# A decode step on one core: projections and output rows summed by weighted adds on ScalarE and DVE, the first K in halves

## The chip, the core and the metric

The kernel runs on one core of one Trainium2 chip. It computes one decoding step: a layer norm, attention with 32 heads over a cache of 16384 keys, and a gated GELU block beside it, for a batch of one. The metric is the device time of one execution in microseconds (us), the median over runs. All data is fp32.

## The reference

```python
xn = layernorm(x)                                   # x: 1 x 576
q = (xn @ wq).reshape(32, 128)                      # wq: 576 x 4096
scores = q_h . k_cache[h] * 128 ** -0.5             # k_cache: 32 x 16384 x 128
o_h = softmax(scores_h) @ v_cache[h]                # v_cache: 32 x 16384 x 128
attn = concat(o_h) @ wo                             # wo: 4096 x 576
h = gelu_tanh(xn @ w_gate) * (xn @ w_up)            # both 576 x 4608
out = x + attn + h @ w_down                         # w_down: 4608 x 576
```

The caches are 268 MB each, the five weight matrices together some 51 MB.

## The kernel before

There are three large SBUF slots of 64 KB in each partition: `sa`, `sb` and `sv` (slot_a, slot_b and slot_v in the profile). One head's K or V fills a slot: partition p holds 128 keys of 128 numbers each. All large transfers are issued on SP's queue, in program order; a transfer into a slot waits there until the slot's readers are done, and so does everything behind it on SP. The class `Order` works out the semaphore waits of the parts that are not in loops from the byte ranges that instructions read and write; an instruction of DVE waits for an earlier one of DVE too where the two share bytes that one of them writes. The helpers `pe_op` (L207), `dve` (L210), `act` (L215) and `load` (through L107) record those instructions, so all of them carry these lines in the profile.

**Start.** The 576 rows of a projection lie as four rows of 128 partitions (row j of partition p is weight row 4p+j) and a tail of 64 weight rows, each split in two over 128 partitions. SP loads wq (into `sa`), its tail (`sb`), then row 3 and the tail of w_gate and of w_up (`sv`), then the other three rows of w_gate (`sb`), of w_up (`sa`, after the q projection), K of head 0 (`sb`), K of head 1 (`sa`) and V of head 0 (`sv`). `project` multiplies on PE: the normalised x, copied to 32 columns, is the stationary operand, one step for each of the four rows and the tail, accumulated in PSUM. q takes 40 matmuls, w_gate and w_up 60 each. `ffn` then takes the diagonal parts out of PSUM with DVE (`tensor_mul` with `same`, `tensor_reduce`) and `ffn_act` makes `hT`, the 4608 hidden numbers as 128 x 36.

**Heads.** For each head DVE multiplies K by q in place (L382), reduces over the 128 numbers of a key (L384), and finds the maximum with PE's help (L387, L389); ScalarE takes the exponent; PE multiplies by V (L329, 32 matmuls). DVE's mul and reduce free K's slot for K two heads later, PE's end frees V's slot for the next V.

**Tail.** w_down lies as 36 rows of 576 numbers in each partition, wo as 32. `WD_A` = 28 rows of w_down go to `sb` once head 30's K has been used; V of head 31 is issued behind them; once head 31's K has been used, 8 more rows of w_down and the first 20 rows of wo go to `sa`, and 12 rows of wo to `sb`, in the pieces of `WO_PIECES`. DVE adds the 28 rows, each times a column of `hT`, into one row `total`: one `tensor_scalar` and 27 `scalar_tensor_tensor`, each on the result of the one before. PE multiplies `total` by ones, the other 8 rows by columns of `hT`, and the 32 rows of wo by columns of `oT`, the normalised attention output; the first 24 rows of wo go in two halves of 288 columns, the last 8 in four quarters of 144. x comes in through `x2`. A copy by DVE (`o4`) and four small stores end the kernel.

Of the kernel before, what the change touches and what calls it, by code (L numbers as in the profile page):

```python
# [9 lines left out]
AF = mybir.ActivationFunctionType  # L10
ALU = mybir.AluOpType
# [19 lines left out]
WD_A = 28  # L31
WO_PIECES = (8, 12, 4, 4, 2, 1, 1)
WO_A = 20
WO_Q = 8
QUART = D // 4
SLOT_AT = 27904
# [117 lines left out]
def decode(tc, x, k_cache, v_cache, wq, wo, wg, wu, wd, out, slots, s_ends):  # L154
    nc = tc.nc
    o = Order(tc)
    places = [e.mark_branch_hint_location() for e in (nc.vector, nc.scalar)]
# [29 lines left out]
    x2 = sbuf("x2", P, HALF)  # L187
# [4 lines left out]
    lsum, oall = sbuf("lsum", P, H), sbuf("oall", P, H + 1)  # L192
# [4 lines left out]
    oT = sbuf("oT", P, WO_T)  # L197
    assert nc.sbuf_base <= SLOT_AT, nc.sbuf_base

# [13 lines left out]
    def act(out, src, func=AF.Copy, signal=None, **kw):  # L213
        also = [kw["accum_out"]] if "accum_out" in kw else []
        o.op("scalar", lambda e: e.activation(out, src, func, **kw), out, src, kw.get("bias") if isinstance(kw.get("bias"), bass.AP) else None, also=also, signal=signal)  # L215
# [5 lines left out]
    ROW3 = 3 * DF  # L221
    nc.tensor.wait_ge(s_ends, 64).then_inc(s_ends, -64)
    qt = load(sb[:, ROW3 : ROW3 + QS], wtail["q"])
    row3, tails, at = {}, {}, 0
    for n in "gu":
        row3[n] = load(sv[:, at : at + DF], wmain[n][:, ROW3:])
        tails[n] = load(sv[:, at + DF : at + DF + DF // 2], wtail[n])
        at += DF + DF // 2

    xrow = sv[:1, ROW3 + FG : ROW3 + FG + D]  # L230
    load(xrow, xf, eng="scalar")
    o.op("gpsimd", lambda e: e.memset(x2, 0.0), x2)
    for i in range(2):
        load(x2[32 * i : 32 * i + 1, :], xf[:, i * HALF : (i + 1) * HALF], eng="scalar")
# [5 lines left out]
    s_q, s_m, s_n, s_o, s_e, s_v, s_po, s_pq, s_pt, s_pb, s_pc, s_vf, s_kf, s_qf, s_qd, s_d, s_a = (  # L240
        tc.alloc_semaphore(f"h{n}") for n in range(17))
    s_k = [tc.alloc_semaphore(f"k{n}") for n in range(2)]
    for bank, s in ((PO, s_po), (pc, None), (pq, None)):
        o.op("vector", lambda e, bank=bank: e.memset(bank, 0.0), bank, signal=s)
# [15 lines left out]
    for j in range(DJ):  # L260
        pe_op(pc[:, j : j + 1], xm[:, j, :], ones[:1, :1], True, True)
    xd = sv[:1, ROW3 + 2 * FG : ROW3 + 2 * FG + 2 * (D - DM)]
    dve("tensor_copy", xd.rearrange("o (d s) -> o d s", s=2), xrow[:, DM:].unsqueeze(2).to_broadcast([1, D - DM, 2]))
    pe_op(pc[:, DJ : DJ + 1], xd, ones[:1, :1], True, True)
    xp = small[:, 26 : 26 + DJ + 1]
    dve("tensor_copy", xp, pc[:, : DJ + 1])
    xnb, xtb = z[:, : DJ * 32], z[:, DJ * 32 : DJ * 32 + 64]
    dve("tensor_copy", xnb.rearrange("p (j r) -> p j r", j=DJ), xp[:, :DJ].unsqueeze(2).to_broadcast([P, DJ, 32]))
    xt = tt[:, :2]
    dve("tensor_scalar", xt, par, xp[:, DJ:], None, op0=ALU.mult)  # L270
    dve("tensor_copy", xtb.rearrange("p (s r) -> p s r", s=2), xt.unsqueeze(2).to_broadcast([P, 2, 32]))

    def project(dst, steps, group, sizes):
        for k, (j, rhs) in enumerate(steps):
            for b, size in enumerate(sizes):
                for q in range(4):
                    lo = q * group + sum(sizes[:b])
                    if j < DJ:
                        lhs = xnb[:, 32 * j : 32 * j + 32]
                    else:  # L280
                        lhs = xtb[:, 32 * (q // 2) : 32 * (q // 2) + 32]
                        lo -= q // 2 * 2 * group
                    pe_op(dst[32 * q : 32 * q + 32, 512 * b : 512 * b + size], lhs, rhs[:, lo : lo + size],
                          k == 0, k == len(steps) - 1)

    project(qb, [(DJ, qt)] + [(j, sa[:, j * HD : (j + 1) * HD]) for j in range(DJ)], QG, (QB, QB))
# [10 lines left out]
    def ffn(which):  # L297
        n, t = "gu"[which], (sb, sa)[which]
        steps = [(3, row3[n]), (DJ, tails[n])]
        load(t[:, :ROW3], wmain[n][:, :ROW3])  # L300
        project(pg, steps + [(j, t[:, j * DF : (j + 1) * DF]) for j in range(DJ - 1)], FG, FB)
        gm = sv[:, ROW3 : ROW3 + FG].rearrange("p (m t) -> p m t", t=WD_T)
        at = 0
        for b, size in enumerate(FB):
            m = size // WD_T
            dve("tensor_mul", gm[:, at : at + m, :], pg[:, 512 * b : 512 * b + size].rearrange("p (m t) -> p m t", t=WD_T),
                same[:, at : at + m].unsqueeze(2).to_broadcast([P, m, WD_T]))
            at += m
        dve("tensor_reduce", gu[:, which * WD_T : (which + 1) * WD_T], gm.rearrange("p m t -> p t m"), axis=AX.X, op=ALU.add)

    ffn(0)
    ffn(1)

# [10 lines left out]
    def out_steps(h):  # L324
        return [(pc[:, :1], z[:, j * DH : (j + 1) * DH], same[:, j : j + 1], j == 0, j == 3) for j in range(4)]
# [12 lines left out]
    ffn_act()  # L338
    o.wait("tensor", [ident, ones, same], [pg, pc, PO, pq])
    o.wait("vector", [qs], [S, pm, nm])  # L340
    o.wait("scalar", [qb], [z, qs, nb, pe, lsum, oall, qcur])

# [6 lines left out]
    for h, dst in ((0, sb), (1, sa)):  # L349
        o.wait("sync", [], [dst])  # L350
        load_k(h, dst, h)
# [9 lines left out]
    with nc.Fori(0, H, engines=OrderedEngineSet([KIND["tensor"]]), head_slot={KIND["tensor"]: 0}):  # L361
# [6 lines left out]
        take(nc.tensor, s_o)  # L368
        chain(out_steps(0), s_pc)
# [4 lines left out]
        nc.tensor.drain().then_inc(s_vf, 1)  # L374

    with nc.vector.Fori(0, H // 2):
        for s, kt in ((0, sb), (1, sa)):
            blk = kt.rearrange("p (n d) -> p n d", d=DH)
            sc = S[:, s * R : s * R + R]
            take(nc.vector, s_k[s], 16)  # L380
            take(nc.vector, s_qd)
            nc.vector.tensor_mul(blk, blk, qs.unsqueeze(1).to_broadcast([P, R, DH])).then_inc(s_d, 1)  # L382
            nc.vector.wait_ge(s_d, 1).then_inc(s_qf, 1)
            nc.vector.tensor_reduce(sc, blk, axis=AX.X, op=ALU.add).then_inc(s_d, 1)  # L384
            nc.vector.wait_ge(s_d, 2).then_inc(s_kf, 1)
            take(nc.vector, s_d, 2)
            nc.vector.reduce_max(pm, sc, axis=AX.X).then_inc(s_m, 1)  # L387
            take(nc.vector, s_pt)
            nc.vector.tensor_reduce(nm[:1], pt[:1, :P], axis=AX.X, op=ALU.max, negate=True).then_inc(s_n, 1)  # L389

    for h0, n in ((0, 6), (6, 8), (14, 8), (22, 8), (30, 2)):
        row, lo = divmod(min(h0 + 2, H - 1), H // 4)
        with nc.scalar.Fori(0, n) as i:
            take(nc.scalar, s_po)
            nc.scalar.activation(z, PO, AF.Copy).then_inc(s_o, 1)  # L395
# [7 lines left out]
            take(nc.scalar, s_pc)  # L403
            nc.scalar.activation(oall[:, bass.ds(i + h0, 1)], pc[:, :1], AF.Copy)
            src = q_part(min(h0 + 2, H - 1)) if n == 2 else qb[32 * row : 32 * row + 1, bass.ds(i * DH + lo * DH, DH)]
            nc.scalar.activation(qcur, src, AF.Copy).then_inc(s_q, 1)

# [5 lines left out]
    first = load_rows(sb, 0, wdv, 0, WD_A)  # L413
    total = first[0]
    dve("tensor_scalar", total, total, hT[:, 0:1], None, op0=ALU.mult)
    for j in range(1, WD_A):
        dve("scalar_tensor_tensor", total, first[j], hT[:, j : j + 1], total, op0=ALU.mult, op1=ALU.add)
# [3 lines left out]
    wd_rows = load_rows(sa, 0, wdv, WD_A, WD_T - WD_A)  # L421
    wo_rows, lo = [], 0
    for n in WO_PIECES:
        wo_rows += load_rows(sa, WD_T - WD_A + lo, wov, lo, n) if lo < WO_A else load_rows(sb, 1 + lo - WO_A, wov, lo, n)
        lo += n

    take(nc.scalar, s_po)
    act(z, PO)
    o.note("scalar", o.sem["scalar"], o.count["scalar"], [pc, pq, pb, PO, qb], [oall, lsum])
    for s in out_steps(H - 1):  # L430
        pe_op(*s)
    act(oall[:, H:], pc[:, :1])

# [4 lines left out]
    dve("tensor_mul", on, oall[:, 1:], rl)  # L438
# [6 lines left out]
    seen = set()  # L445
    pairs = (qb[:, :512], qb[:, 512:])
    acc4 = pg[:, :QUART]
    half = [[pairs[i][32 * (2 * i + j) : 32 * (2 * i + j) + 1, :HALF] for j in range(2)] for i in range(2)]
    quart = [acc4[32 * g : 32 * g + 1, :] for g in range(4)]

    def add_out(groups, lhs, w, last=False):
        n = D // len(groups)
        for i, g in enumerate(groups):
            pe_op(g, lhs, w[:, i * n : (i + 1) * n], id(g) not in seen, last)
            seen.add(id(g))

    turn = 0
    for w, lhs in [(w, hT[:, WD_A + j : WD_A + j + 1]) for j, w in enumerate(wd_rows)] + [(total, ones[:, :1])]:
        add_out(half[turn % 2], lhs, w)
        turn += 1  # L460
    for j, w in enumerate(wo_rows):
        if j < WO_T - WO_Q:
            add_out(half[turn % 2], oT[:, j : j + 1], w, last=j >= WO_T - WO_Q - 2)
            turn += 1
            continue
# [42 lines left out]
```

## Time and profile before

| | |
|---|---|
| median of 3 runs | 1365.26 us (1364.94 to 1365.76) |
| the profiled execution's own time | 1364.84 us |
| its span, first to last instruction | 1363.0 us |
| DVE busy | 1158.4 us, 85% |
| PE busy | 446.3 us, 33% |
| ScalarE busy | 67.8 us, 5% |
| mean granted TensorE clock | 0.629 of full speed |
| HBM read | 587.60 MB |

The span leaves out 1.84 us of the profiled execution's time, so a span is compared with a span, and 1.84 us and the distance to the median are added at the end. Times of day in the text are us from the start of the span. In a timeline row the first number is the start, the second the length; the brackets at its end hold the idle time of the engine before it and what ended that. Rows with xN stand for N instructions. PE records two matmuls for one fp32 matmul. SPq rows are the issues of transfers, not the transfers.

### The profile page before, as it was taken

The page shows a single profiled execution, that of the slowest core. Times are in us where ns is not written, and L with a number is a line of the kernel's source. Part 1 is how long each engine was busy: PE and PEld are TensorE (multiplying, and loading weights), DVE is VectorE, ACT ScalarE, POOL GpSimd, SP SyncE. Part 2 cuts the span into 40 slices and gives each one's busy share as a digit, 9 for nine tenths or more (in the row PEclk, how much of TensorE's full clock was granted, in tenths as well). Part 3 has the DMA queues.
Part 4 walks back from the last instruction along what each step waited for, and adds up shares of the span by engine and source line. Part 5 has one row for each costly group of instructions (what it writes and reads, how often), then busy time and mean ns, then how long its engine had stood idle before and what let it go on. Part 6 is the DMA issues. An engine that isn't in the chain of part 4 may idle for free. (4 is left out here: it accounts for less than half of the span.)

```text
span 1363.0 us, 7778 instructions
## 1 busy us (share of the span) xinstructions
PE 446.3 (33%) x3012; PEld 161.7 (12%) x3012; DVE 1158.4 (85%) x193; ACT 67.8 (5%) x234; POOL 1.0 (0%) x7
## 2 busy tenths in 40 slices
PE   2431233333322333323222333333223333232236
PEld 1110101111111111101111111011011111011112
DVE  1049999999998888898888888998888888988882
ACT  0000000000000000000000000000000000000000
POOL 0000000000000000000000000000000000000000
PEclk9675666666556666665566666665566666655568
DMA  9999999999999999999999999999999999999998
GB/s 401 446 424 431 431 440 437 431 435 431 435 437 431 433 431 431 446 435 431 431 439 433 433 431 431 446 435 431 431 435 437 433 431 431 444 437 431 430 437 349
DMA packets 11683, 587.69 MB, mean 431 GB/s; under 512 B 1303, under 2 KB 1309, under 8 KB 1694
## 3 DMA queue, kind: packets, MB, share of 16 engines
q1 hardware_dynamic: 11668, 587.60, 99.7%
q8 instruction: 5, 0.08, 0.0%
q10 hardware_dynamic: 10, 0.01, 0.0%
HBM read 587.60 MB, written 0.00 MB: 431 GB/s over the span
## 5 line engine op out<-in xcount | busy, mean ns | idle before, releaser
L329 PE MATMUL po<-slot_v,pe 128*4 128x512 f32 x2048 | 291.7, 733 | 532.6 <-PEq L333 532.6
L382 DVE TENSOR_TENSOR slot_b<-slot_b,qs 128x16384 f32<-128x16384 f32 x16 | 275.6, 17226 | 38.0 <-DVEq L333 38.0
L382 DVE TENSOR_TENSOR slot_a<-slot_a,qs 128x16384 f32<-128x16384 f32 x16 | 275.6, 17226 | 30.6 <-DVEq L333 30.6
L384 DVE TENSOR_REDUCE scores<-slot_a 128x128 f32<-128x16384 f32 x16 | 275.5, 17220 | 2.3
L384 DVE TENSOR_REDUCE scores<-slot_b 128x128 f32<-128x16384 f32 x16 | 275.5, 17220 | 2.3
L329 PEld LDWEIGHTS po<-slot_v,pe 128*4 128x4 f32 x2048 | 56.2, 98 | 740.9 <-issue 740.9
L365 PE MATMUL pg<-ident,pm 128*1 128x128 f32 x32 | 11.9, 371 | 287.3 <-PEq L333 287.3
L329 PE MATMUL pc<-same,z 128*128 128x1 f32 x256 | 59.8, 355 | 0.0
L395 ACT ACTIVATE z<-po 128x512 f32<-128x512 f32 x32 | 19.1, 597 | 783.1 <-ACTq L333 783.1
L329 PEld LDWEIGHTS pc<-same,z 128*128 128x128 f32 x256 | 57.1, 328 | 0.5
L210 DVE TENSOR_TENSOR slot_v<-pg,same 128x396 f32<-128x396 f32 (+1 forms) x6 | 3.3, 558 | 51.9 <-PE pg L207 51.7
L365 PEld LDWEIGHTS pg<-ident,pm 128*1 128x1 f32 x32 | 2.5, 79 | 292.6 <-issue 292.6
L389 DVE TENSOR_REDUCE nm<-pg 1x1 f32<-1x128 f32 x32 | 8.9, 279 | 21.5 <-DVEq L333 21.5
L329 PE MATMUL pg<-nm,ones 1*128 1x1 f32 x64 | 17.7, 343 | 18.5 <-PEq L333 18.5
L329 PE MATMUL pqs<-qcur,ones 1*128 1x128 f32 x64 | 14.8, 312 | 25.3 <-PEq L333 25.3
L210 DVE SCALAR_TENSOR_TENSOR slot_b<-slot_b,hT 128x576 f32<-128x576 f32 x27 | 22.1, 819 | 0.9
L400 ACT ACTIVATE nb<-pg 128x1 f32<-128x1 f32 x32 | 5.5, 171 | 292.3 <-ACTq L333 292.3
L329 PEld LDWEIGHTS pg<-nm,ones 1*128 1x128 f32 x64 | 15.9, 306 | 27.9 <-issue 27.9
L387 DVE TENSOR_REDUCE pm<-scores 128x1 f32<-128x128 f32 x32 | 9.1, 286 | 8.2 <-DVEq L333 8.2
L329 PEld LDWEIGHTS pqs<-qcur,ones 1*128 1x128 f32 x64 | 9.6, 186 | 53.9 <-issue 53.9
L207 PE MATMUL pg<-slot_b,z 128*32 128x396 f32 (+1 forms) x72 | 8.8, 661 | 17.5 <-DMA slot_b<-in_B_w_gate_dram 17.5
L402 ACT ACTIVATE pe<-scores,nb 128x128 f32 x32 | 12.8, 401 | 9.6 <-ACTq L333 9.6
(79 smaller groups left out, 115.3 us busy)
## 6 DMA issues: line engine op xcount, KB each, us to landing
slot_b<-in_B_w_down_dram SPq DMA_DIRECT2D x1, 8064.0 KB, 42.0
slot_b<-in_B_w_gate_dram SPq DMA_DIRECT2D x1, 6912.0 KB, 54.9
slot_a<-in_B_w_up_dram SPq DMA_DIRECT2D x1, 6912.0 KB, 38.2
slot_a<-in_A_wo_dram SPq DMA_DIRECT2D x1, 3456.0 KB, 41.0
slot_v<-in_B_w_gate_dram SPq DMA_DIRECT2D x1, 2304.0 KB, 28.8
slot_v<-in_B_w_up_dram SPq DMA_DIRECT2D x1, 2304.0 KB, 36.8
slot_a<-in_B_w_down_dram SPq DMA_DIRECT2D x1, 2304.0 KB, 28.1
slot_a<-in_A_wo_dram SPq DMA_DIRECT2D x1, 2304.0 KB, 33.2
```

Source lines behind the costliest of these rows:

```text
L207: o.op("tensor", lambda e: e.matmul(outp, lhsT, rhs, start=start, stop=stop), outp, lhsT, rhs, signal=signal)
L210: o.op("vector", lambda e: getattr(e, name)(out, *ins, **kw), out, *[a for a in ins if isinstance(a, bass.AP)], *[a for a in kw.values() i ...
L329: i = nc.tensor.matmul(dst, lhs, rhs, start=start, stop=stop)
L365: nc.tensor.transpose(pt[:1, :P], pm, ident).then_inc(s_pt, 1)
L382: nc.vector.tensor_mul(blk, blk, qs.unsqueeze(1).to_broadcast([P, R, DH])).then_inc(s_d, 1)
L384: nc.vector.tensor_reduce(sc, blk, axis=AX.X, op=ALU.add).then_inc(s_d, 1)
L387: nc.vector.reduce_max(pm, sc, axis=AX.X).then_inc(s_m, 1)
L389: nc.vector.tensor_reduce(nm[:1], pt[:1, :P], axis=AX.X, op=ALU.max, negate=True).then_inc(s_n, 1)
L395: nc.scalar.activation(z, PO, AF.Copy).then_inc(s_o, 1)
L400: nc.scalar.activation(nb, pb[:, :1], AF.Copy, scale=SCALE).then_inc(s_a, 1)
L402: nc.scalar.activation(pe, S[:, bass.ds(i % 2 * R, R)], AF.Exp, bias=nb, scale=SCALE, accum_out=lsum[:, bass.ds(i + h0, 1)]).then_inc(s_e, 1)
```

## The change

The projections are summed by weighted adds: ScalarE (`weigh`) scales one of the four rows in place by its column of x, DVE (`gather`) adds the other rows and the two halves of the tail onto it, and PE only sums over partitions, with `ones` as the stationary operand (8 matmuls for q, 12 each for w_gate and w_up). ScalarE copies the result out of PSUM into `gm` (`unfold`), DVE takes the diagonal there (`fold`). w_gate's three rows are issued ahead of w_up's row 3 and tail; w_up's three rows come in two transfers. K of head 0 comes in two halves, and DVE works on each; `fold(1)` and `ffn_act` come behind head 0's reduces. DVE's loop covers heads 1 to 30, and head 31 stands behind it.

In the tail `WD_A` is 20, and 16 further rows of w_down come in two pieces of 8 behind V of head 31. DVE adds all 36 rows of w_down and 22 of the 32 rows of wo, in turn into two accumulators `totals`; PE takes eight rows of wo in halves (`WO_HALF`), which DVE adds to `totals[1]`, and the last two rows, with the sum of the totals, in quarters. x comes in through `xres`.

In PE's loop `out_steps` moves behind the 32 matmuls with V, and ScalarE's copies `z` and `oall` move to the end of its loop. PE gets a branch hint and a `release` as DVE and ScalarE had.

```diff
-WD_A = 28
-WO_PIECES = (8, 12, 4, 4, 2, 1, 1)
-WO_A = 20
-WO_Q = 8
+WD_A = 20
+WD_B = (8, 8)
+WO_PIECES = (4, 8, 8, 4, 4, 2, 1, 1)
+WO_A = 12
+WO_HALF = (5, 7, 9, 11, 13, 15, 17, 19)
+WO_QUART = 2
...
-    nc.tensor.wait_ge(s_ends, 64).then_inc(s_ends, -64)
...
+        if n == "g":
+            load(sb[:, : 3 * DF], wmain[n][:, : 3 * DF])
...
+    def weigh(total, j):
+        act(total, total, scale=xp[:, j : j + 1])
+
+    def gather(total, steps):
+        for j, row in steps:
+            n = row.shape[1]
+            for s in range(2) if j == DJ else (0,):
+                part = total[:, s * n : (s + 1) * n]
+                col = xt[:, s : s + 1] if j == DJ else xp[:, j : j + 1]
+                dve("scalar_tensor_tensor", part, row, col, part, op0=ALU.mult, op1=ALU.add)
+
+    def project(dst, total, group, sizes):
+        for b, size in enumerate(sizes):
+            for q in range(4):
+                lo = q * group + sum(sizes[:b])
+                pe_op(dst[32 * q : 32 * q + 32, 512 * b : 512 * b + size], ones[:, :32], total[:, lo : lo + size], True, True)
...
+    nc.scalar.wait_ge(s_ends, 64).then_inc(s_ends, -64)
+    weigh(qrows[0], 0)
+    gather(qrows[0], [(j, qrows[j]) for j in range(1, DJ)] + [(DJ, qt)])
+    project(qb, qrows[0], QG, (QB, QB))
+    weigh(rows["g"][0], 3)
...
+    gather(rows["g"][0], [(DJ, tails["g"])] + [(j, rows["g"][1 + j]) for j in range(3)])
+    project(pg, rows["g"][0], FG, FB)
+    weigh(rows["u"][0], 3)
+    unfold(0)
+    gather(rows["u"][0], [(DJ, tails["u"])])
+    fold(0)
+    gather(rows["u"][0], [(j, rows["u"][1 + j]) for j in range(3)])
+    project(pg, rows["u"][0], FG, FB)
+    unfold(1)
...
+    for src, sc in parts:
+        blk = src.rearrange("p (n d) -> p n d", d=DH)
+        dve("tensor_mul", blk, blk, qs.unsqueeze(1).to_broadcast([P, SUB, DH]))
+        dve("tensor_reduce", sc, blk, axis=AX.X, op=ALU.add)
...
+    fold(1)
+    ffn_act()
...
-    first = load_rows(sb, 0, wdv, 0, WD_A)
+    wd_rows = load_rows(sb, 0, wdv, 0, WD_A)
     take(nc.sync, s_vf)
     load_v(H - 1)
     take(nc.sync, s_kf)
+    for n in WD_B:
+        wd_rows += load_rows(sa, len(wd_rows) - WD_A, wdv, len(wd_rows), n)
+    totals, turn = wd_rows[:2], 0
+
+    def add_row(row, col):
+        nonlocal turn
+        total, turn = totals[turn % 2], turn + 1
+        if total is row:
+            dve("tensor_scalar", total, row, col, None, op0=ALU.mult)
+        else:
+            dve("scalar_tensor_tensor", total, row, col, total, op0=ALU.mult, op1=ALU.add)
+
+    for j, row in enumerate(wd_rows):
+        add_row(row, hT[:, j : j + 1])
+        if j == 1:
+            dve("tensor_add", totals[0][:1], totals[0][:1], xres)
...
+    for j, row in enumerate(wo_rows):
+        col = oT[:, j : j + 1]
+        if j in WO_HALF:
+            add_out(half, col, row, j == WO_HALF[0], j == WO_HALF[-1])
+        elif j < WO_T - WO_QUART:
+            add_row(row, col)
+        if j == WO_PIECES[0] + WO_PIECES[1] + WO_PIECES[2] + WO_PIECES[3] - 1:
+            for i, g in enumerate(half):
+                part = totals[1][:1, i * HALF : (i + 1) * HALF]
+                dve("tensor_add", part, part, g)
+        if j == WO_T - WO_QUART - 1:
+            dve("tensor_add", totals[0], totals[0], totals[1])
+        if j == WO_T - 2:
+            add_out(quart, col, row, True, False)
+            add_out(quart, ones[:, :1], totals[0], False, False)
+        elif j == WO_T - 1:
+            add_out(quart, col, row, False, True)
```

More of the change, by code (lines that the diff above doesn't have):

```diff
@@ L197, in decode @@
     oT = sbuf("oT", P, WO_T)
+    gm = sbuf("gm", P, FG)
     assert nc.sbuf_base <= SLOT_AT, nc.sbuf_base
@@ L266, in decode @@
+    xp, xt = small[:, 26 : 26 + DJ + 1], tt[:, :2]
     dve("tensor_copy", xp, pc[:, : DJ + 1])
-    xnb, xtb = z[:, : DJ * 32], z[:, DJ * 32 : DJ * 32 + 64]
-    dve("tensor_copy", xnb.rearrange("p (j r) -> p j r", j=DJ), xp[:, :DJ].unsqueeze(2).to_broadcast([P, DJ, 32]))
-    xt = tt[:, :2]
     dve("tensor_scalar", xt, par, xp[:, DJ:], None, op0=ALU.mult)
[L271 to L284, printed above, removed]
@@ new lines, in project, with unfold, fold @@
+    def project(dst, total, group, sizes):
[3 more added lines that the diff above has]
+                pe_op(dst[32 * q : 32 * q + 32, 512 * b : 512 * b + size], ones[:, :32], total[:, lo : lo + size], True, True)
+    def unfold(which):
+        at = 0
+        for b, size in enumerate(FB):
+            act(gm[:, at : at + size], pg[:, 512 * b : 512 * b + size])
+            at += size
+    def fold(which):
+        g3 = gm.rearrange("p (m t) -> p m t", t=WD_T)
+        dve("tensor_mul", g3, g3, same.unsqueeze(2).to_broadcast([P, 32, WD_T]))
+        dve("tensor_reduce", gu[:, which * WD_T : (which + 1) * WD_T], gm.rearrange("p (m t) -> p t m", t=WD_T), axis=AX.X, op=ALU.add)
@@ L295, in decode @@
     act(qcur, q_part(1), signal=s_q)
[L297 to L312, printed above, removed]
+    for lo, hi in ((0, 2), (2, 3)):
+        load(sa[:, lo * DF : hi * DF], wmain["u"][:, lo * DF : hi * DF])
+    rows["u"] += [sa[:, j * DF : (j + 1) * DF] for j in range(3)]
+    gather(rows["g"][0], [(DJ, tails["g"])] + [(j, rows["g"][1 + j]) for j in range(3)])
[7 more added lines that the diff above has]
+    unfold(1)
     def ffn_act():
@@ L336, in head @@
         return bass.ds(h, 1)
[L338 to L341, printed above, removed]
     def load_k(h, dst, s):
@@ L359, in decode, with highest, scores_of @@
             load_v(i * 2 + (1 + s))
-    with nc.Fori(0, H, engines=OrderedEngineSet([KIND["tensor"]]), head_slot={KIND["tensor"]: 0}):
+    def highest(sc):
+        nc.vector.reduce_max(pm, sc, axis=AX.X).then_inc(s_m, 1)
+        take(nc.vector, s_pt)
+        nc.vector.tensor_reduce(nm[:1], pt[:1, :P], axis=AX.X, op=ALU.max, negate=True).then_inc(s_n, 1)
+    def scores_of(kt, s):
+        sc = S[:, s * R : s * R + R]
+        blk = kt.rearrange("p (n d) -> p n d", d=DH)
+        take(nc.vector, s_k[s], 16)
+        take(nc.vector, s_qd)
+        nc.vector.tensor_mul(blk, blk, qs.unsqueeze(1).to_broadcast([P, R, DH])).then_inc(s_d, 1)
+        nc.vector.wait_ge(s_d, 1).then_inc(s_qf, 1)
+        nc.vector.tensor_reduce(sc, blk, axis=AX.X, op=ALU.add).then_inc(s_d, 1)
+        nc.vector.wait_ge(s_d, 2).then_inc(s_kf, 1)
+        take(nc.vector, s_d, 2)
+        highest(sc)
+    take(nc.vector, s_qd)
+    for src, sc in parts:
+        blk = src.rearrange("p (n d) -> p n d", d=DH)
+        dve("tensor_mul", blk, blk, qs.unsqueeze(1).to_broadcast([P, SUB, DH]))
+        dve("tensor_reduce", sc, blk, axis=AX.X, op=ALU.add)
+    nc.vector.wait_ge(o.sem["vector"], o.count["vector"]).then_inc(s_kf, 1)
+    nc.vector.nop().then_inc(s_qf, 1)
+    o.wait("tensor", [ident, ones, same], [pg, pc, PO, pq])
+    o.wait("scalar", [qb], [z, qs, nb, pe, lsum, oall, qcur])
+    fold(1)
+    ffn_act()
+    o.wait("vector", [qs], [S, pm, nm])
+    highest(S[:, :R])
+    with nc.Fori(0, H, engines=OrderedEngineSet([KIND["tensor"]])):
         take(nc.tensor, s_q)
@@ L374, in decode @@
         nc.tensor.drain().then_inc(s_vf, 1)
[L376 to L389, printed above, removed]
+        take(nc.tensor, s_o)
+        chain(out_steps(), s_pc)
+    with nc.vector.Fori(0, (H - 2) // 2):
+        scores_of(sa, 1)
+        scores_of(sb, 0)
+    scores_of(sa, 1)
     for h0, n in ((0, 6), (6, 8), (14, 8), (22, 8), (30, 2)):
@@ L443, in decode, with add_out @@
     act(oT, po)
[L445 to L451, printed above, removed]
+    half = [qb[32 * i : 32 * i + 1, 512 * i : 512 * i + HALF] for i in range(2)]
+    quart = [pg[32 * i : 32 * i + 1, :QUART] for i in range(4)]
+    def add_out(groups, lhs, w, first, last):
@@ L452, in add_out @@
         n = D // len(groups)
         for i, g in enumerate(groups):
[L454 to L465, printed above, removed]
-        if j == WO_T - 4:
-            dve("tensor_add", x2[:64], x2[:64], pairs[1][64:, :HALF])
-            dve("tensor_add", x2[:64], x2[:64], pairs[0][:64, :HALF])
-            for i, g in enumerate(quart):
-                r, lo = 32 * (i // 2), i % 2 * QUART
-                pe_op(g, ones[r : r + 1, :1], x2[r : r + 1, lo : lo + QUART], False, False)
-        add_out(quart, oT[:, j : j + 1], w, last=j == WO_T - 1)
+            pe_op(g, lhs, w[:, i * n : (i + 1) * n], first, last)
```

85 lines of the change are left out of this document (36 added, 49 removed).

## The prediction

> **What bounds the kernel now.** The page comes first: the busy share of the DMA engines in 40 slices, and the queue that SP fills.
>
> ```profile
> DMA  9999999999999999999999999999999999999998
> q1 hardware_dynamic: 11668, 587.60, 99.7%
> ```
>
> The transfers are busy throughout. Whether they ever ran dry is read from landings: PE begins on a V that it waited for, and DVE on a K.
>
> ```profile
> 172.57 9.44 PE L329 MATMUL po<-slot_v,pe 128*4 128x512 f32 x64 [2.86 <-PEq L333]
> ...
> 1293.54 8.75 PE L329 MATMUL po<-slot_v,pe 128*4 128x512 f32 x64 [19.26 <-PEq L333]
> ...
> 1331.88 8.35 PE L329 MATMUL po<-slot_v,pe 128*4 128x512 f32 x64 [18.96 <-PEq L333]
> ```
>
> V of head 1 lands at 172.5, V of head 30 at 1293.5: 29 heads of 16.78 MB in 1121.0 us, 434 GB/s and 38.65 us a head. V of head 31 follows 38.3 us later, behind 28 rows of w_down (8.26 MB) and its own 8.39 MB: the same rate. So the stream is dense here, and only its two ends can move. The chain that ended last shows the far end.
>
> ```profile
> 1323.32 35.86 DMA slot_b<-in_A_wo_dram
> 1359.18 0.04 issue
> 1359.22 0.55 PE pg L207 x8
> 1359.77 0.02 issue
> 1359.79 0.31 DVE z L210
> ```
>
> The last row of wo lands at 1359.18, 3.8 us before the span's end: 0.59 us for PE to finish with it, and 3.23 us from there (copy, stores, the end). PE and DVE keep up with the transfers. That is the measure for the change: it moves the same bytes, with the same last pieces (4, 4, 2, 1, 1 rows), so I leave the last landing at 1359.2 and ask whether the start starves the queue and whether the tail still keeps up.
>
> **The start.** These rows bound it.
>
> ```profile
> 22.92 2.42 PE L207 MATMUL pc<-ones,slot_v 1*128 1x1 f32 x10 [22.92 <-PEq L222]
> 26.32 3.64 PE L207 MATMUL qb<-slot_b,z 128*32 128x512 f32 x16 [0.98 <-DVE z L210]
> 59.15 8.79 PE L207 MATMUL pg<-slot_b,z 128*32 128x396 f32 x72 [17.49 <-DMA slot_b<-in_B_w_gate_dram]
> 75.54 7.43 PE L207 MATMUL pg<-slot_a,z 128*32 128x396 f32 x72 [3.73 <-DMA slot_a<-in_B_w_up_dram]
> 83.69 2.17 DVE L210 TENSOR_REDUCE gu<-slot_v 128x36 f32<-128x1152 f32 x1
> 95.06 17.23 DVE L382 TENSOR_TENSOR slot_b<-slot_b,qs 128x16384 f32<-128x16384 f32 x1 [7.92 <-DVEq L333]
> L210 DVE SCALAR_TENSOR_TENSOR slot_b<-slot_b,hT 128x576 f32<-128x576 f32 x27 | 22.1, 819 | 0.9
> L210 DVE TENSOR_TENSOR tt<-gu 128x36 f32<-128x36 f32 x1 | 0.2, 186 | 0.0
> L382 DVE TENSOR_TENSOR slot_b<-slot_b,qs 128x16384 f32<-128x16384 f32 x16 | 275.6, 17226 | 38.0 <-DVEq L333 38.0
> L395 ACT ACTIVATE z<-po 128x512 f32<-128x512 f32 x32 | 19.1, 597 | 783.1 <-ACTq L333 783.1
> L398 ACT ACTIVATE qs<-pqs 128x128 f32<-128x128 f32 x32 | 8.9, 277 | 49.8 <-ACTq L333 49.8
> ```
>
> From the 36 and the 16384 wide multiply, an element costs DVE (17226-186)/16348 = 1.042 ns. The weighted add of 576 takes 819 ns: 600 for the elements and 219 fixed; with the 0.9 us of idle time before the 27 of them, one that needs the one before starts (22.1+0.9)/27 = 0.853 us after it. ScalarE costs (597-277)/384 = 0.83 ns an element, so 3.6 us for 4096.
>
> wq is there by 22.9 (PE waited for it). New: ScalarE's scaling to 26.5; three adds of 4096, 3 x 4.52 = 13.6, to 40.1; two of 2048, 4.7, to 44.8; PE's 8 matmuls, 3.64 as the 16 records above, to 48.4. Then SP may issue w_up's main rows. The queue ahead of them is covered until 59.15, where w_gate's main rows landed: 10.7 us of cover. w_gate: its tail, 2 x 2.62, to 50.0; its main rows now stand ahead of 3.54 MB of w_up, so they land at 59.15-8.15 = 51.0; three adds of 4608 at 5.05, to 66.2. K's halves for head 0 are issued at 61.1 and 66.2, covered until w_up's main rows land at 75.5. Then w_up's tail, 5.2, to 71.4; `fold(0)`, 1.36 for a multiply of 1152 and 2.2 as the reduce above, to 75.0; three adds, to 90.2. There K of head 1 is issued, covered by K of head 0 until 95.06: 4.9 us. V follows PE's sum by some 4 us, with K of head 1 (19.3 us) in front of it. So DVE is busy some 40 us where PE was, and it costs nothing as long as this cover holds; it is thinnest at K of head 1.
>
> DVE starts on head 0 at 90.2 instead of 95.06, its four half steps take 4 x 8.7, to 125.0, then `fold(1)` (1.36 and 2.2) and `ffn_act` (five of some 0.2 and ScalarE's), some 5 us, to 130.
>
> ```profile
> 130.00 0.34 SPq L344 DMA_DIRECT2D slot_b<-in_A_k_cache_dram  x1
> ...
> 1274.33 17.22 DVE L382 TENSOR_TENSOR slot_a<-slot_a,qs 128x16384 f32<-128x16384 f32 x1 [2.55 <-DVEq L333]
> ```
>
> So head 1 starts as before; only K of head 2 is issued some 5 us sooner than 130.00, ahead of a queue that holds V of head 0 until 133.4 (95.06+38.3) either way: nothing gained. Later DVE idles 2.55 us before a K; the move of `out_steps` and of ScalarE's copies (1 to 2 us) is hidden in such gaps. The heads: 0.
>
> **The tail.** Here the change puts 56 weighted adds on DVE's one queue.
>
> ```profile
> 1309.07 0.33 SPq L107 DMA_DIRECT2D slot_a<-in_B_w_down_dram  x1
> 1310.14 0.28 DVE L389 TENSOR_REDUCE nm<-pg 1x1 f32<-1x128 f32 x1 [0.67 <-DVEq L333]
> ...
> 1342.38 0.36 DVE L210 RECIPROCAL small<-pg 128x32 f32<-128x32 f32 x1 [6.28 <-PE pg L207]
> 1343.00 0.29 DVE L210 TENSOR_TENSOR z<-tt,quarter 128x128 f32<-128x128 f32 x1
> 1343.35 0.41 PE L207 MATMUL pg<-same,z 128*128 128x32 f32 x2 [1.00 <-DVE z L210]
> 1343.79 0.20 ACT L215 ACTIVATE oT<-pg 128x32 f32<-128x32 f32 x1 [1.42 <-PE pg L207]
> 1350.94 3.09 PE L207 MATMUL qb<-slot_a,oT 128*1 128x288 f32 x48 [1.04 <-DMA slot_a<-in_A_wo_dram]
> ```
>
> Landings: a row of 128x576 (0.295 MB) takes 0.68 us at 434 GB/s. The first 20 rows of w_down land at 1293.5+13.6 = 1307.1, V of head 31 at 1326.4, the next 8 rows at 1331.9 (just where V landed before, the bytes up to there being equal), 8 more at 1337.3; wo as before, row 19 at 1350.9, rows 20 to 23 by 1353.8. V is issued when PE is done with head 30's, at 1293.54+8.75 = 1302.3, covered until 1307.1; the rest at 1309.1, covered until 1326.4.
>
> DVE is free at 1310.4 and done with the first 20 rows by 1326 to 1328: then it must wait until 1331.9. From there 16 rows of w_down, the reciprocal group, 22 rows of wo and three sums stand on it in program order, and the first row of wo needs `oT`. Its pace decides. Consecutive adds now go to two totals, so each needs only the one before the last. How closely such instructions follow each other is shown here only by small ones.
>
> ```profile
> 3.50 0.23 DVE L210 TENSOR_REDUCE par<-ident 128x2 f32<-128x128 f32 x1
> 3.65 0.35 DVE L210 TENSOR_REDUCE same<-ident 128x32 f32<-128x128 f32 x1
> 25.58 0.23 DVE L210 COPY z<-small 128x128 f32<-128x128 f32 x1
> 25.72 0.22 DVE L210 TENSOR_SCALAR tt<-par,small 128x2 f32<-128x2 f32 x1
> ```
>
> The second of each pair begins 0.08 to 0.09 us before the first ends. For the add that makes 0.819-0.08 = 0.74 us a row. Bounds: 0.853 with no overlap, 0.60 with nothing but the elements. I take 0.74, the nearest rows' overlap.
>
> The Trainium skill, "Vector Engine (DVE) Microarchitecture Reference", section "Measured stream behaviour on trn2", gives about 75 ns an instruction beside the elements after queue overlap; by that a row would be 0.675 us, an estimate, and the sum below some 1 us less, since DVE then waits for rows 20 to 23. The trace's 36 wide multiply, 186 ns less 37 for its elements and 80 of overlap, agrees; whether a column as the scalar adds to it no row shows.
>
> The sum, on the clock of the profiled execution:
> - rows of w_down from 1331.95: 16 x 0.74 = 11.85, to 1343.8;
> - reciprocal group, 1342.38 to 1343.29 above, 0.91, to 1344.7; PE and ScalarE until `oT` is read, 1343.29 to 1344.05, 0.75, to 1345.45 (PE and ScalarE are through with head 31 by some 1338, five us earlier than before);
> - 16 rows of wo, 11.85, to 1357.3 (the last four landed at 1353.8);
> - two sums out of PSUM, 0.45 each, 0.9, to 1358.2;
> - 6 rows, 4.45, to 1362.65; the last result 0.1; sum of the totals, 0.60 + 0.15 = 0.75, to 1363.5;
> - PE: the four matmuls with the total, then the last row's four, behind them in its queue: 0.43 and 0.55 at the clock of before, at most twice that where the clock has gone to half; I take 1.4, to 1364.95;
> - copy and stores 3.23: 1368.2.
>
> ```profile
> L210 DVE TENSOR_TENSOR x<-x,qb 64x288 f32<-64x288 f32 x2 | 0.9, 452 | 11.9 <-PE qb L207 11.8
> 1357.51 0.42 PE L207 MATMUL pg<-x,ones 1*1 1x144 f32 x8
> ```
>
> The stores at the end now wait for DVE instead of the last transfer: 1368.2-1363.0 = +5.2 us. The start's and the heads' terms are 0. From the profiled execution 1370.0, from the median 1370.5; I forecast 1370.3.
>
> **The rivals.**
> - *No overlap.* Every add waits out the one before: 38 rows at 0.853 add 4.2 us to the sum, +9.4, 1374.7. For it: all 27 adds of before stand at that distance. Against: each of those needed the last one's result. The skill, "VectorE: DVE Perf Modes", section "The DRAIN you can't avoid", says that the next operation does not start until the pipe is empty and that leaving out semaphores gained nothing in its test; by it this rival is right. The starts at 3.65 and 25.72 above speak against it.
> - *DVE keeps pace (the other side).* At 0.617 us a row or less DVE overtakes the transfers and waits for wo's rows 20 to 23 at 1353.8. From that point: 4 rows 2.5, two sums of 288 elements 0.6, 6 rows 3.7, sum 0.75, PE at full clock 0.9, 3.23: 1365.5, +2.5, 1367.8, which is not slower than before by more than a measurement can tell. For it: the elements alone are 0.60. Against: every pair above keeps part of its fixed cost.
> - *K of head 1 comes too late.* If the start's sums take over 4.9 us longer than worked out, the queue runs dry at 95.06 and everything shifts by the excess; 5 us more than that makes 1375.3. Against: all its durations are measured slopes.
> - *A faster kernel* would need the stream itself to end earlier and DVE to keep pace. The stream delivers 23.6 MB by 59.15, which take 54.4 us at 434 GB/s, so 4.8 us lie in its start-up. Nothing that I see in the change shortens it; should it save all, 1363.
>
> **How the numbers follow.** Forecast 0.62, no overlap 0.18, DVE keeps pace 0.13, K late 0.04, faster 0.03. The likeliest's own range is 1368.3 to 1372 (a row from 0.66 to 0.78, PE from 1.0 to 2.0). For 8 in 10 it reaches down to the kept pace and up to the no-overlap one: 1367.5 to 1375.0. About 0.2%, 2.7 us, is what a measurement here can tell from no change, so slower begins at 1368.0: slower 0.62+0.18+0.04 = 0.84 less 0.01 of the forecast's lower edge, 0.83; same 0.14; faster 0.03.
>
> **What would show it.** Starts of consecutive adds 0.74 us apart in the tail; DVE with no gap over 1 us from 1332 on except for `oT`; the last landing still near 1359.2, some 4 us before the sum of the totals ends; a chain of waits that ends in DVE instead of a DMA. K of head 1 issued near 90 and V of head 1 at PE near 172.5 show the start free. The prediction is wrong if the last landing moves by over 1 us, if the adds stand 0.85 apart, or if DVE waits for rows of wo.

## The result, and the profile after

The changed kernel takes 1373.07 us (1372.23 to 1373.62, 6 runs), the kernel before beside it 1365.54 us (1364.94 to 1366.46, 6 runs): the ratio is 1.0053, with a 95% interval of 1.004 to 1.0066. It is 7.5 us slower, where 5.2 were forecast. Its profiled execution took 1373.62 us, with a span of 1371.6 us against 1363.0. That execution is the slowest of its six, so its trace is a little long against the median.

The page of the changed kernel shows the transfers still busy almost throughout, and another chain at the end.

```profile
DMA  9999999999999999999999999999999999999996
...
q1 hardware_dynamic: 12244, 587.60, 99.2%
...
DVE 2%; DMA 2%; issue 0%; PE 0%; ACT 0%; DVEq 0%
```

Before, the chain went from DMA to PE's last rows. Now it leaves the transfers with the first piece of w_down behind V of head 31, and from there runs on DVE. These are its pieces (start, length, what):

```profile
1311.16 24.34 DMA slot_a<-in_B_w_down_dram
...
1335.60 5.46 DVE slot_b L213 x8
...
1348.23 0.65 PE pg L210 x2
...
1361.47 1.97 DVE slot_b L213 x4
...
1366.33 0.77 DVE slot_b L213
1367.10 0.04 issue
1367.14 1.26 PE pg L210 x16
1368.40 0.02 issue
1368.42 0.31 DVE z L213
```

The same stretch in DVE's timeline shows its pace, and where it waited.

```profile
1314.06 13.21 DVE L213 SCALAR_TENSOR_TENSOR slot_b<-slot_b,hT 128x576 f32<-128x576 f32 x18
1335.60 11.76 DVE L213 SCALAR_TENSOR_TENSOR slot_b<-slot_a,hT,slot_b 128x576 f32<-128x576 f32 x16 [8.32 <-DMA slot_a<-in_B_w_down_dram]
...
1349.14 5.92 DVE L213 SCALAR_TENSOR_TENSOR slot_b<-slot_a,oT,slot_b 128x576 f32<-128x576 f32 x8 [0.96 <-ACT oT L218]
...
1361.85 4.44 DVE L213 SCALAR_TENSOR_TENSOR slot_b<-slot_b,oT 128x576 f32<-128x576 f32 x6
```

It idles 8.32 us for the transfer before the 16 rows, 0.96 for `oT`, and for no transfer after that, though narrowly: rows 20 to 23 of wo landed at 1357.60, and DVE began on them at 1357.89. With 0.815 us for one add (the page's mean), 16 adds in 11.76 us start (11.76-0.815)/15 = 0.730 us apart. From the landing at 1335.50 to the span's end pass 36.1 us; the forecast had 36.3. So the tail came out as worked out. But its start is 3.6 us late: the forecast has the piece at 1331.9. The rows of wo behind it are late too, as PE's wait for the last but one shows:

```profile
1362.61 0.66 PE L210 MATMUL pg<-slot_b,oT 128*1 128x144 f32 x8 [5.64 <-DMA slot_b<-in_A_wo_dram]
```

The last row lands at 1363.30, where the kernel before had it at 1359.18. The landings of V, read at PE, show where that comes from (heads 8, 30 and 31; the first row is the kernel before, whose other two stand in the prediction):

```profile
443.51 8.80 PE L329 MATMUL po<-slot_v,pe 128*4 128x512 f32 x64 [19.27 <-PEq L333]
```

```profile
443.85 9.03 PE L341 MATMUL po<-slot_v,pe 128*4 128x512 f32 x64 [21.18 <-PEq L345]
...
1295.68 9.78 PE L341 MATMUL po<-slot_v,pe 128*4 128x512 f32 x64 [21.18 <-PEq L345]
...
1330.13 9.62 PE L341 MATMUL po<-slot_v,pe 128*4 128x512 f32 x64 [16.93 <-PEq L345]
```

From head 8 to head 30 the kernel before takes (1293.54-443.51)/22 = 38.638 us a head, the changed one (1295.68-443.85)/22 = 38.720. That small difference is 2.1 us at head 30. Then V of head 31 comes 34.45 us later, although only 14.29 MB lie between, 32.9 us at 434 GB/s: another 1.5 us. Both losses are in a stream that the forecast took as fixed.

The start in DVE's and SP's timelines:

```profile
50.02 15.13 DVE L213 SCALAR_TENSOR_TENSOR slot_v<-slot_b,small,slot_v 128x4608 f32<-128x4608 f32 x3
...
73.59 15.12 DVE L213 SCALAR_TENSOR_TENSOR slot_v<-slot_a,small,slot_v 128x4608 f32<-128x4608 f32 x3
88.62 8.68 DVE L213 TENSOR_TENSOR slot_b<-slot_b,qs 128x8192 f32<-128x8192 f32 x1
```

```profile
88.79 0.33 SPq L351 DMA_DIRECT2D slot_a<-in_A_k_cache_dram  x1
93.08 0.33 SPq L354 DMA_DIRECT2D slot_v<-in_A_v_cache_dram  x1
123.68 0.35 SPq L351 DMA_DIRECT2D slot_b<-in_A_k_cache_dram  x1
```

K of head 1 goes out at 88.79 (forecast 90.2, needed before 95.06), K of head 2 at 123.68 (forecast 125.0, before the change 130.00).

### The profile page after: what moved, and what is told of

Read it like the earlier page. It is cut to its first block, busy times and chain, and to the rows that moved or that the text cites. A ratio compares the mean times of both kernels' runs of the same rounds, so it can differ in the third digit from the quotient of the medians.

```text
span 1371.6 us, 7003 instructions
## 1 busy us (share of the span) xinstructions
PE 393.8 (29%) x2595; PEld 122.4 (9%) x2595; DVE 1235.3 (90%) x234; ACT 81.6 (6%) x241; POOL 0.7 (0%) x6
## 5 line engine op out<-in xcount | busy, mean ns | idle before, releaser
L381 DVE TENSOR_TENSOR slot_a<-slot_a,qs 128x16384 f32<-128x16384 f32 x16 | 275.6, 17225 | 33.0 <-DVEq L345 32.9
L381 DVE TENSOR_TENSOR slot_b<-slot_b,qs 128x16384 f32<-128x16384 f32 x15 | 258.4, 17225 | 31.4 <-DVEq L345 31.4
L383 DVE TENSOR_REDUCE scores<-slot_b 128x128 f32<-128x16384 f32 x15 | 258.3, 17220 | 2.2
L341 PE MATMUL pc<-same,z 128*128 128x1 f32 x256 | 32.8, 249 | 28.9 <-PEq L345 28.9
L341 PEld LDWEIGHTS pc<-same,z 128*128 128x128 f32 x256 | 31.0, 191 | 57.7 <-issue 57.7
L213 DVE SCALAR_TENSOR_TENSOR slot_a<-slot_a,small 128x4096 f32<-128x4096 f32 x3 | 13.5, 4485 | 12.8 <-ACT slot_a L218 12.8
L213 DVE SCALAR_TENSOR_TENSOR slot_b<-slot_a,hT,slot_b 128x576 f32<-128x576 f32 x16 | 11.8, 815 | 8.3 <-DMA slot_a<-in_B_w_down_dram 8.3
L210 PE MATMUL pg<-slot_v,ones 128*32 128x396 f32 (+1 forms) x48 | 8.1, 842 | 35.9 <-DVE slot_v L213 35.9
L213 DVE TENSOR_REDUCE scores<-slot_b 128x64 f32<-128x8192 f32 x2 | 17.4, 8686 | 0.1
L213 DVE TENSOR_TENSOR slot_b<-slot_b,qs 128x8192 f32<-128x8192 f32 x2 | 17.4, 8683 | 0.0
```

The source lines that it names most:

```text
L210: o.op("tensor", lambda e: e.matmul(outp, lhsT, rhs, start=start, stop=stop), outp, lhsT, rhs, signal=signal)
L213: o.op("vector", lambda e: getattr(e, name)(out, *ins, **kw), out, *[a for a in ins if isinstance(a, bass.AP)], *[a for a in kw.values() i ...
L341: i = nc.tensor.matmul(dst, lhs, rhs, start=start, stop=stop)
```

## The experiments

Times are medians; they were taken in two groups, with the kernel before beside each. Beside the kernel before at 32736, the changed kernel at 32256, one total and the start alone it took 1365.69 us (25 runs); beside the other four, 1365.89 us (23 runs). The theory for the tail was that of the forecast: DVE's queue of dependent work ends after the transfers. For the slower stream the suspects were the slots' address in the partition, which the change moves from byte 27904 to 32736, and the rearranged loops with DVE's additional work.

**The kernel before with the slots at 32736.**

```diff
-SLOT_AT = 27904
+SLOT_AT = 32736
```

> The kernel before with one constant changed: the three slots begin at byte 32736 of each partition, as in the changed kernel, instead of 27904. 32736 is 511.5 x 64, 27904 is 436 x 64. In the changed kernel's trace V of heads 8 and 30 land 851.83 us apart, 38.720 us a head, against 38.638 before. Theory: the slots' address does that; then the heads here take 38.72 us each, V of head 30 reaches PE some 2 to 2.5 us after 1293.5, and the time is 2 to 3 us above the kernel before. Rival: the new order in the heads' loops or DVE's new work does it; then V of head 30 stays at 1293.5 and the time within 0.5 us of the kernel before.

1367.83 us (11 runs), 2.1 above the kernel before; ratio 1.0018, interval 1.0009 to 1.0027. V of heads 8 and 30 at PE:

```profile
445.61 9.87 PE L329 MATMUL po<-slot_v,pe 128*4 128x512 f32 x64 [19.38 <-PEq L333]
...
1297.44 8.92 PE L329 MATMUL po<-slot_v,pe 128*4 128x512 f32 x64 [19.38 <-PEq L333]
```

(1297.44-445.61)/22 = 38.720 us, the changed kernel's pace to the last digit, with the old loops. The address does it. (V of head 30 stands 3.9 us behind, not 2 to 2.5; 2.1 of that were there at head 8 already, and 2.0 at head 1, whose V comes at 174.55 instead of 172.57. This profiled execution took 1369.02 us, more than most of the eleven.)

**The changed kernel with the slots at 32256.**

```diff
-SLOT_AT = 32736
+SLOT_AT = 32256
```

> The changed kernel with the slots at byte 32256, which is 504 x 64, instead of 32736; nothing else. If the address slows the transfers: 38.64 us a head and 2 to 3 us less than the changed kernel, 1370 to 1371 where the changed kernel gave 1373.07. If the loops' order does it: 38.72 us a head and 1373.

1369.31 us (9 runs), 3.8 below the changed kernel, more than the 2 to 3 expected. Heads 8, 30 and 31:

```profile
442.53 9.69 PE L341 MATMUL po<-slot_v,pe 128*4 128x512 f32 x64 [21.06 <-PEq L345]
...
1292.55 9.63 PE L341 MATMUL po<-slot_v,pe 128*4 128x512 f32 x64 [21.07 <-PEq L345]
...
1326.28 9.84 PE L341 MATMUL po<-slot_v,pe 128*4 128x512 f32 x64 [16.12 <-PEq L345]
```

38.637 us a head: the old pace, with the new loops. V of head 31 comes 33.73 us behind head 30's, 0.8 more than its bytes need, where the changed kernel lost 1.5. So some 2.4 us of the 3.8 are the pace of the heads and 0.7 the wait before V of head 31, which need not be the address's doing (the run with one total, below, has the address and not the wait). The remaining 0.7 lies outside the spans: their medians, 1370.25 and 1367.2, stand 3.05 apart.

**The kernel before with the slots at 27936**, to part the 32 bytes from the place.

```diff
-SLOT_AT = 27904
+SLOT_AT = 27936
```

> The kernel before with the slots at byte 27936, 32 bytes behind where they were; 27936 is 436.5 x 64. If it is the 32 bytes by which the slots miss a multiple of 64 that slow the transfers, the heads take 38.72 us each as at 32736. If it is where in the partition the slots lie, 38.64 us.

1367.56 us in its one run, which alone would say little; the pace is what counts. V of head 8 at 443.74 and of head 30 at 1295.56:

```profile
443.74 8.70 PE L329 MATMUL po<-slot_v,pe 128*4 128x512 f32 x64 [19.40 <-PEq L333]
...
1295.56 9.45 PE L329 MATMUL po<-slot_v,pe 128*4 128x512 f32 x64 [19.39 <-PEq L333]
```

38.719 us a head, 32 bytes from a place that gives 38.638. Two starts at a multiple of 64 bytes give 38.64, two that miss it by 32 give 38.72. Both fast starts are multiples of 128 and of 256 as well, so which of these counts no run parts.

**One total.** From the third row on all adds go to the first total, so each waits for the one before.

```diff
-        total, turn = totals[turn % 2], turn + 1
+        total, turn = totals[0 if turn > 1 else turn], turn + 1
```

> The changed kernel, but from the third row on every weighted add goes to the first total, so that each waits for the one before it; the same number of adds. By the forecast's account DVE's pace ends the tail: starts 0.853 us apart instead of 0.735, 38 adds behind the first piece of w_down on V, so 38 x 0.118 = 4.5 us more than the changed kernel, 1377.5. If the waits for the transfers set the tail's pace and not DVE, under 1 us more.

1376.81 us (4 runs), 3.7 above the changed kernel. The 16 rows of w_down behind V:

```profile
1334.39 13.63 DVE L213 SCALAR_TENSOR_TENSOR slot_b<-slot_a,hT,slot_b 128x576 f32<-128x576 f32 x16 [4.73 <-DMA slot_a<-in_B_w_down_dram]
```

With 0.82 us for one, (13.63-0.82)/15 = 0.854 us apart, against 0.730. From the landing (1334.35) to the span's end (1374.6) pass 40.25 us instead of 36.1: 4.15 of the 4.5 expected, the landing itself being 1.15 us earlier here. DVE's pace sets the tail, and two totals save 0.12 us a row.

The landing is earlier because V of head 31 lost nothing here. PE was done with head 30's V in 8.77 us instead of 9.78, and V of head 31 went out sooner:

```profile
1328.93 9.33 PE L341 MATMUL po<-slot_v,pe 128*4 128x512 f32 x64 [15.47 <-PEq L345]
```

Head 30's stands at 1295.93. That is 33.00 us for the 14.29 MB, where the changed kernel took 34.45.

**The start alone.** The changed start and heads with the tail of before (and the slots at 32256); the diff against the changed kernel, cut:

```diff
-SLOT_AT = 32736
+SLOT_AT = 32256
-WD_A = 20
-WD_B = (8, 8)
-WO_PIECES = (4, 8, 8, 4, 4, 2, 1, 1)
-WO_A = 12
+WD_A = 28
+WO_PIECES = (8, 12, 4, 4, 2, 1, 1)
+WO_A = 20
+WO_Q = 8
-    xres = sbuf("xres", 1, D)
+    x2 = sbuf("x2", P, HALF)
...
+    first = load_rows(sb, 0, wdv, 0, WD_A)
+    total = first[0]
...
+    for w, lhs in [(w, hT[:, WD_A + j : WD_A + j + 1]) for j, w in enumerate(wd_rows)] + [(total, ones[:, :1])]:
+        add_out(half[turn % 2], lhs, w)
```

> The changed kernel's start, heads and K in halves, with the tail of the kernel before (28 rows of w_down added by DVE in one chain, all other rows on PE, x through x2) and the slots at byte 32256. By the forecast's account the start and the heads cost nothing: within 0.5 us of the kernel before, V of head 30 near 1293.5, a chain of waits that ends in the transfers of wo. If the sums on DVE and ScalarE at the start cost something, it shows here: V of head 1 at PE later than 172.6 by that much, and the time above the kernel before by the same.

1364.18 us (11 runs): 1.5 below the kernel before, ratio 0.9989, interval 0.998 to 0.9998. It beats both kernels, the kernel before by little: the interval is 0.3 to 2.7 us. The end of its chain of waits, and V of head 30:

```profile
1322.30 36.13 DMA slot_b<-in_A_wo_dram
1358.44 0.04 issue
1358.48 0.55 PE pg L208 x8
```

```profile
442.50 9.24 PE L341 MATMUL po<-slot_v,pe 128*4 128x512 f32 x64 [21.06 <-PEq L345]
...
1292.54 9.18 PE L341 MATMUL po<-slot_v,pe 128*4 128x512 f32 x64 [21.07 <-PEq L345]
```

The chain ends in the transfers again, 0.7 us sooner; V of head 30 is 1.0 us earlier than before, and V of head 8 too (442.50 against 443.51), though the pace behind head 8 is the same. The start doesn't cost: it gains, and what the trace shows of the gain lies ahead of head 8. Against this kernel, the changed kernel with its slots at 32256 shows the tail alone: 1369.31-1364.18 = 5.1 us.

**K of head 0 in one piece**, in the start-only kernel, to see what gained there.

```diff
-SUB = 64
+SUB = 128
```

> The start-only kernel (1364.18, 1.5 us below the kernel before) with K of head 0 in one transfer and DVE's work on it in one piece (SUB 128 instead of 64). The forecast held that the halves gain nothing, because K of head 2 is issued ahead of a queue that is covered either way. If that is right, 1364.2 still. If the earlier issue of K of head 2 (123.5 instead of 130.0) is what gained, DVE waits here for the whole K until some 94.5, K of head 2 goes out at 129 and, with the gate's and the activation's work now behind it on DVE, K of head 3 some 5 us later than in the kernel before, close to the end of the queue: some transfer engines run dry and the time is 1 to 5 us above the start-only kernel.

1366.31 us (11 runs), 2.1 above the start-only kernel, or 1.9 when each is held against the kernel before beside it. SP's issues of K for heads 2 and 3, and V of head 8 at PE, here:

```profile
128.52 0.34 SPq L351 DMA_DIRECT2D slot_b<-in_A_k_cache_dram  x1
145.98 0.34 SPq L354 DMA_DIRECT2D slot_v<-in_A_v_cache_dram  x1
169.37 0.33 SPq L351 DMA_DIRECT2D slot_a<-in_A_k_cache_dram  x1
```

```profile
443.79 9.12 PE L341 MATMUL po<-slot_v,pe 128*4 128x512 f32 x64 [18.05 <-PEq L345]
```

In the start-only kernel the issues of K go out at 123.47 and 164.31, and V of head 8 comes 1.3 us earlier. The trace also holds the time at which each of the 16 parts of a transfer is done, and these completions tell the two issues apart. K of head 2 is complete at 152.79 here and at 152.71 in the start-only kernel, so its later issue cost at most 0.1 us. K of head 3 was issued at 169.37, ahead of a V of head 1 that was complete at 172.09 (PE began on it only at 172.86, behind ScalarE's exponent, which ended at 172.47). The first part of that V was done at 170.44 already, and K of head 3 came 20.29 us behind it instead of 19.30 for the same bytes. So 1.0 of the 1.3 us are the late issue of K of head 3.

**28 rows ahead of V of head 31 again**, with the slots at 32256.

```diff
-WD_A = 20
-WD_B = (8, 8)
+WD_A = 28
+WD_B = (8,)
```

> The changed kernel with the slots at byte 32256 and WD_A 28, WD_B (8,): 28 rows of w_down ahead of V of head 31 again instead of 20. In the run with only the slots moved, V of head 31 reached PE 33.7 us after V of head 30, where 14.29 MB take 32.9 at 434 GB/s. Theory: V was issued so close to the end of the 20 rows that some of the transfer engines ran dry; with 28 rows V of head 31 comes 38.4 us after V of head 30, with nothing lost. DVE then adds 28 rows while V comes in and only 8 behind it, so its tail starts up to 1.2 us sooner: 1368.2, against 1369.3. If the 0.8 us are not lost there but by the smaller pieces, V comes 39.1 us after and the time gains 0.4 us at most.

1370.03 us (1368.68 to 1371.14, 7 runs): no gain over 1369.31 (1368.79 to 1370.79). The first half of the expectation holds, the second fails:

```profile
1330.94 9.94 PE L341 MATMUL po<-slot_v,pe 128*4 128x512 f32 x64 [20.77 <-PEq L345]
```

```profile
1336.36 5.92 DVE L213 SCALAR_TENSOR_TENSOR slot_b<-slot_a,hT,slot_b 128x576 f32<-128x576 f32 x8 [4.12 <-DMA slot_a<-in_B_w_down_dram]
1343.66 0.36 DVE L213 RECIPROCAL small<-pg 128x32 f32<-128x32 f32 x1 [1.38 <-PE pg L210]
```

V of head 31 comes 38.36 us after head 30's (1292.58): nothing is lost, so the 0.8 us were the thin cover. But V comes 4.7 us later, PE is through with head 31 that much later, and DVE, done with its 8 rows at 1342.3, waits 1.38 us for PE. What the order gave it took back there.

**The last 10 rows of wo on PE**, on top of that.

```diff
-WO_QUART = 2
+WO_QUART = 10
-        if j == WO_PIECES[0] + WO_PIECES[1] + WO_PIECES[2] + WO_PIECES[3] - 1:
+        if j == WO_T - WO_QUART - 1:
...
-        if j == WO_T - 2:
-            add_out(quart, col, row, True, False)
+        if j >= WO_T - WO_QUART:
+            add_out(quart, col, row, j == WO_T - WO_QUART, j == WO_T - 1)
+        if j == WO_T - 3:
             add_out(quart, ones[:, :1], totals[0], False, False)
-        elif j == WO_T - 1:
-            add_out(quart, col, row, False, True)
```

> As the run before it (slots at 32256, 28 rows ahead of V of head 31), and the last 10 rows of wo on PE in quarters instead of the last 2, so that DVE adds 14 rows of wo instead of 22 and its sum of the totals comes before the last transfer. By the forecast's account the tail costs only because DVE's queue ends after the transfers: 14 rows from 1344.5 end at 1354.8, the sums at 1356.6, before the last row at 1358.4; then the chain ends in the transfers again and the time is that of the start-only run, 1364.2. If PE's cold clock or the sums themselves cost it, some 2 us more.

1364.88 us (11 runs), 5.2 below the kernel with 2 rows on PE; ratio to the kernel before 0.9993, interval 0.9984 to 1.0002. The chain leaves DVE:

```profile
1326.50 30.39 DMA slot_b<-in_A_wo_dram
1356.90 0.04 issue
1356.94 2.70 PE pg L210 x40
```

DVE's sum of the totals ends at 1357.6 (forecast for it 1356.6), PE then has 40 records in one stretch behind a late row and ends at 1359.64, where the start-only kernel ends at 1359.03. That is the difference between the two, 0.7 us, or 0.5 when each is held against the kernel before beside it: 8 rows moved off DVE's queue take away all but this of the tail's cost.

## Why the prediction was right or wrong

- *The tail*, the term that carried the forecast: right in mechanism, and in size as far as DVE's queue goes. From the landing to the span's end it measured 36.1 us against 36.3, with an add every 0.730 us against 0.74, the reciprocal group 0.90 against 0.91, the way to `oT` 0.97 against 0.75 (PE's two records take 0.65 instead of 0.41), the two sums 0.85, the last sum 0.77, and PE 1.26 against 1.4. Between the two kernels that differ in the tail lie 5.1 us, where 5.2 were forecast; that this is so close is partly luck, since 0.8 of the 5.1 were lost by V of head 31, which the forecast put at nothing.
- *The overlap.* The rival without any would need 0.853; the run with one total shows that value, and 4.15 us for it, so it is what the second total avoids. The Trainium skill's figure that the forecast named ("Vector Engine (DVE) Microarchitecture Reference", section "Measured stream behaviour on trn2") would give 0.675, an estimate; the trace has 0.730 for an add whose scalar is a column, so here the measurement decides, some 55 ns above it. The Trainium skill's other rule ("VectorE: DVE Perf Modes", section "The DRAIN you can't avoid") is borne out only for adds that need the one in front; the same paragraph adds that an operation which is not held starts earlier, and the adds with two totals did (0.730 us apart at a length of 0.815).
- *DVE keeps pace.* It did not, but the border was nearer than the forecast's 0.617 us a row. Before rows 20 to 23 stand 28 adds, 16 of w_down and 12 of wo, so it is (1353.8-1331.95-0.91-0.75)/28 = 0.72. The measured 0.730 lies just above, and DVE met those rows 0.29 us after they landed.
- *The start.* Its durations were right to 1.4 us over 66 us of DVE, and K of head 1 did not start late. But the step "nothing gained" for the earlier K of head 2 was wrong. It counted the cover of the queue as a whole: V of head 0 until 133.4, so an issue at 130.00 seemed in time. The completions show that the first part of that V was done at 131.63, and K of head 2 came 0.2 us later than its bytes need (1.8 and 0.0 us in the two executions of the kernel before with the slots moved). The term was put at 0 and measured 1.5 us of gain in the medians, start and heads together. The trace shows 1.0 of them at head 8: about 0.25 when K of head 2 is complete (152.96 against 152.71), the rest between there and head 8. What makes that rest no run shows.
- *The stream.* "I leave the last landing at 1359.2" was the step that failed, and it is most of the miss. The last landing moved by 4.1 us, and over 1 us was what the prediction itself called a sign of being wrong. The piece of w_down that starts the tail landed 3.6 us late, 2.1 of them by V of head 30 and 1.5 at V of head 31. The first part is the slots' address, which the whole diff changes (the cut one shown ahead leaves the line out) and the forecast passed over; moving it back gains 3.8 us in the changed kernel, 2.4 of them in the heads' pace. The other is V of head 31: "covered until 1307.1" was 4.8 us on paper, with 8.75 us for PE on head 30's V. PE took 9.78 and was done only at 1305.46, V went out at 1305.65, and 1.5 us were lost in this execution (0.8 with the slots at 32256, nothing in the run with one total).
- *The sum.* Start -1.5 (forecast 0), tail +5.1 (forecast +5.2), address +3.8 (not in the forecast) make +7.4, where +7.5 was measured. These are steps through the runs from one kernel to the other, so that they add up tests nothing. The time, 1373.07, lies in the range given for 8 in 10, but above the likeliest case's own 1368.3 to 1372, and it is partly luck that it lies no higher: an error of -1.5 hid part of one of +3.8.
- *The other two rivals.* K of head 1 did not come late: it was issued at 88.79, K of head 0 was complete at 94.10 in the changed kernel, and K of head 1 came 19.35 us behind it, the heads' pace. A faster kernel was put at 0.03 on the ground that nothing in the change shortens the stream; the start-only kernel shows that something does.

## What to carry to other kernels

When the transfers bound a kernel, work handed from PE to DVE near the end must be counted as a queue against the landings: rows behind the last large transfer, times DVE's real distance between instructions, plus everything that stands in the same program order. A second accumulator is worth 0.12 us an add of 576, and no more. An issue a few us ahead of the queue's end is not yet in time: count from where the first parts of the transfer in front are done. And a constant that only moves buffers is part of the change: look at where the buffers start.

## What the runs showed of the hardware that was not expected

Slots that start 32 bytes off a multiple of 64 slow transfers whose rows are 64 KB a partition by 0.2%: 38.72 against 38.64 us for 16.78 MB, in four placements of two kernels. Why, no view here shows.

A queue that looks covered at the issue can still lose time, and the completions in the traces show why. In these rows the 16 parts of a transfer are done 1.6 to 2.1 us apart, and when the next transfer is issued shortly before the first of them is done, fewer than 16 packets are in flight for a while. The last column is how much later than at the heads' pace the transfer was complete.

| execution | transfer | issued | parts in front done, first to last | fewer than 16 packets in flight | later by |
|---|---|---|---|---|---|
| before | K of head 2 | 130.00 | 131.63 to 133.41 | 1.5 us | 0.2 us |
| before, slots at 32736 | K of head 2 | 130.35 | 131.93 to 133.86 | 2.8 us | 1.8 us |
| before, slots at 27936 | K of head 2 | 130.32 | 131.99 to 133.85 | 0.4 us | 0.0 us |
| K in one piece | K of head 3 | 169.37 | 170.44 to 172.09 | 1.7 us | 1.0 us |
| changed | V of head 31 | 1305.65 | 1307.36 to 1309.17 | 2.1 us | 1.5 us |
| changed, slots at 32256 | V of head 31 | 1302.38 | 1304.38 to 1306.02 | 1.1 us | 0.8 us |
| one total | V of head 31 | 1304.88 | 1307.37 to 1309.42 | 0.0 us | 0.0 us |

An issue 2.49 us ahead of the first part lost nothing, and those 1.1 to 2.0 us ahead lost between nothing and 1.8 us. At nearly the same lead (1.58 to 1.67 us in the first three rows) the loss differs from execution to execution, so a thin cover also makes the time uncertain.

A late issue is not the only thing that delays a transfer. In the start-only kernel K of head 2 was issued early, at 123.47, its first part was done 19.31 us behind the first part of V of head 0, as at the heads' pace, and yet its last part came 20.49 us behind that V's last. In between, from 136.39 on, a load of 16 KB of instructions (queue q8 of the page) ran for 0.96 us. In the kernel before the distance between first and last part grows from 0.77 to 1.79 us around such a load at 37.55. That the load causes the delay fits, but no run tests it.
